# Fourteen loads of x, each issued as two transfers, of 108 and of 20 rows

## The chip, the core and the metric

The kernel runs on one core of one Trainium2 chip. The metric is the device time of one execution in microseconds (us). The kernel before takes 314.12 us, the median of three runs (314.06 to 314.76).

## What is computed

Attention over a small set of inducing points, and behind it a mixture step without a gate. All inputs and the output are float32.

```python
# x: (4, 12544, 128), inducing: (32, 128); scale = 1 / sqrt(128)
def mab(q, kv):
    a = softmax(scale * q @ kv.T)
    return a @ kv
h = mab(inducing, x[b])          # (32, 128) for each of the four batches
y = mab(x[b], h)                 # (12544, 128) for each batch
out = maximum(y @ w1, y @ w2) @ w_out      # w1, w2: (128, 1024), w_out: (1024, 128)
```

## The kernel before, in words

**Tiling.** A batch has 12544 rows of x, 98 for each of the 128 partitions. A tile `xn` holds 14 rows of x for each partition (14 x 128 values in float16), so a batch is seven tiles; there are 12 such buffers. `xT` is the same data turned, with the 128 channels on the partitions. In the text load (b, i) is part i of batch b. Batch 0 is cut finer: its parts hold 14, 14, 14, 14, 7, 7, 7, 7, 6, 4, 2 and 2 rows of x per partition. The later batches have seven parts of 14.

**Loads of x.** `load_x` (L213) issues a load from POOL (GpSimd), since the transfer also turns float32 into float16. One load moves 128 rows of the access pattern, one for each partition. Part (0, 0) alone comes over SP in float32 and is cast by DVE and ACT. POOL takes its instructions in order, and an issue is one of them. The framework counts landings with eight semaphores that it deals out to POOL's transfers in turn, so a transfer waits for the landing of the one issued eight before it, when that has not been waited for yet.

**The head (0 to about 25 us).** Only batch 0 is worked on. PE turns each part of x (L292), DVE and ACT copy the result to `xT` (L296, L299), PE makes scores (L308), ACT takes exp (L320), PE sums (L345, L354). Behind the loads of batch 0 POOL issues two halves of w1 and w2 (`relus<-in_moe_w_dram`, L269 and L270), then w_out (L271), and then the seven loads of batch 1. Between the loads of batch 1 stand three computations of POOL: `w21 = w2 - w1` for columns 256 to 511 (L576), the same for columns 512 to 767 (L576 again), and the cast of the second half of w1 to float16 (L585). Their code, in the order of issue:

```python
load_x(1, 0)
difference(nc.vector, 0, 256, 21.0, 0.34)
difference(nc.gpsimd, 256, 512, 21.0, 0.64)
load_x(1, 1)
load_x(1, 2)
difference(nc.gpsimd, 512, 768, 22.9, 0.64)
cast_w1(1)
for i in range(3, 7):
    load_x(1, i)
```

PE needs the first difference for `hwd` of columns 256 to 511 (L517), the second one for columns 512 to 1023 (L535, `rest_hwd`), and the cast for turning w1 (L598, `weights_2`). DVE makes the difference of the last 256 columns (also L576) before L535.

**The main part (about 25 us to the end).** The order of PE's work is a written list of words (`PLAN`), which is not changed by a late operand: PE stops at an instruction whose operand is missing. The large groups are the hidden products and their relu (PE L956, then DVE L900 or ACT L902), the products with w_out (PE L836), and the outputs, scaled by DVE (L871) and stored by SP (L885). In between, for batches 1 to 3, SP turns `xn` to `xT` by DMA (L227), PE and ACT make scores and exp (L385, L397), SP turns the exps (L415), PE sums (L430). POOL works out softmax denominators for some blocks (L697, L701) from exps that SP turned (L688).

**Later loads.** When the last sum of batch b is made, `load_x(b + 1, i)` is called for i = 0 to 6 in one go (L463 and on), the first behind a small copy (`pace`, L218) that makes POOL wait for that sum.

Of the kernel before, what the change touches and what calls it, by code (L numbers as in the profile page):

```python
# [144 lines left out]
def kernel(  # L145
# [9 lines left out]
    nc = tc.nc  # L155
    B, N, C = x.shape
# [20 lines left out]
    xr = x.rearrange("b (p k) c -> b p k c", p=128)  # L177
# [30 lines left out]
    xn_at = {}  # L208
    for b in range(B):
        for i, (k0, n) in enumerate(parts[b]):  # L210
            off = k0 % P1
            xn_at[b, i] = xn_tiles[(7 * b + k0 // P1) % NXN][:, off : off + n, :]

    def load_x(b, i, after=None):
        k0, n = parts[b][i]
        if after is not None:

            nc.gpsimd.tensor_copy(out=pace, in_=after)  # L218
        nc.gpsimd.dma_start(out=xn_at[b, i][:, 0:n, :], in_=xr[b, :, k0 : k0 + n, :])  # L219

    HALVES = 4
    turns_x = [(i, 7 * h, 7) for i in range(HALVES) for h in (0, 1)] + [(i, 0, P1) for i in range(HALVES, 7)]
# [31 lines left out]
    with tc.manual_schedule(engines={ET.PE, ET.DVE, ET.Activation, ET.Pool, ET.SP}):  # L254
# [3 lines left out]
        for lo, hi in ((0, 8), (8, P1)):  # L258
            nc.sync.dma_start(out=xf[:, lo:hi, :], in_=xr[0, :, lo:hi, :])
        nc.sync.dma_start(ind_sb, inducing)  # L260
        load_x(0, 1)
        make_identity(nc, identity16)
        load_x(0, 2)
        make_identity(nc, identity32)
        for i in range(3, len(parts[0])):
            load_x(0, i)
# [829 lines left out]
```

## Time and profile before

| | |
|---|---|
| Median of three runs | 314.12 us (314.06 to 314.76) |
| The profiled execution | 313.17 us, its span 311.4 us |
| PE, ACT, DVE, POOL busy | 98%, 88%, 87%, 41% of the span |
| DMA packets of POOL's transfers (queue q0) | 22.7% of 16 engines' span |
| DMA packets of SP's transfers (queue q1) | 56.3% of 16 engines' span |
| Granted TensorE clock, mean | 0.998 |

The span runs from the first to the last instruction; the profiled execution has 1.77 us around it. Engines are PE (TensorE), PEld (its weight loads), DVE (VectorE), ACT (ScalarE), POOL (GpSimd) and SP (SyncE). A row of a timeline has the start in us from the start of the span, the duration, engine, line, operation, output and inputs, the count of instructions merged into it, and in brackets how long the engine had been idle and what ended that. A DMA row of POOL shows the time that the issue takes on POOL, not the transfer.

### The profile page before, as it was taken

To read this page: it belongs to the slowest core of one execution; us is meant where nothing else is said; L and a number is where in the kernel's file an instruction comes from. 1 tells how busy PE (TensorE), PEld (TensorE's weight loads), DVE (VectorE), ACT (ScalarE), POOL (GpSimd) and SP (SyncE) were. 2 spreads that over 40 slices of the span, in tenths; PEclk is the share of its full clock that TensorE was granted. 3 is DMA by queue.
4 is the path that set the end of the run, shared out by engine and by line. 5 is a ranking of instruction groups with operands and counts; after the bars stand their busy time and mean duration, and the time that the engine had idled before them with its cause. 6 is when DMAs were issued, how large, how long until landed. Compare 5 with 4: busy or idle time off the path is not lost.

```text
span 311.4 us, 12499 instructions
## 1 busy us (share of the span) xinstructions
PE 305.2 (98%) x5306; PEld 239.8 (77%) x5306; DVE 271.0 (87%) x443; ACT 275.5 (88%) x485; POOL 127.0 (41%) x189
## 2 busy tenths in 40 slices
PE   8999999999999999999999999999999999999995
PEld 3876777778877787778777887687878877788885
DVE  2468999999889999999899888998999899999883
ACT  3669999998998989998999999998989899988884
POOL 7373001476610290568500890347023343297300
PEclk9999999999999999999999999999999999999999
DMA  8999999999599999998899999874422532334323
GB/s 207 208 262 200 200 253 179 201 217 213 116 225 244 223 251 192 165 211 241 168 245 215 242 230 237 179 155 139 137 86 103 138 96 98 108 138 120 113 93 121
DMA packets 81336, 55.81 MB, mean 179 GB/s; under 512 B 62816, under 2 KB 66176, under 8 KB 81280
## 3 DMA queue, kind: packets, MB, share of 16 engines
q1 hardware_dynamic: 75312, 41.32, 56.3%
q0 software_dynamic: 5968, 13.70, 22.7%
q8 instruction: 41, 0.67, 0.9%
q14 instruction: 15, 0.12, 0.1%
HBM read 27.28 MB, written 25.69 MB: 170 GB/s over the span
## 4 chain that ended last, share of the span: by engine, by line
PE 89%; DMA 6%; POOL 2%; DVE 2%; issue 1%; POOLq 0%; DVEq 0%
PE psall L836 60%; PE psall L956 22%; DMA xn<-in_x_dram 3%; DMA relus<-in_moe_w_dram 2%; PE psall L644 2%; PE psall L430 1%; PE psall L385 1%; DVE relus L900 1%; DMA eT<-eu 1%; POOL xn L219 1%; POOL w L576 1%; PE psall L546 0%; PE psall L469 0%; DVE m1bd L565 0%; PE psall L852 0%
## 5 line engine op out<-in xcount | busy, mean ns | idle before, releaser
L902 ACT ACTIVATE relus<-psall 128x512 f16<-128x512 f32 (+1 forms) x373 | 234.0, 713 | 21.6 <-PE psall L956 20.1
L900 DVE TENSOR_SCALAR relus<-psall 128x512 f16<-128x512 f32 (+1 forms) x265 | 194.4, 775 | 18.9 <-PE psall L956 17.8
L836 PE MATMUL psall<-woutp,relus 128*128 128x128 f16 x3104 | 202.0, 220 | 0.0
L836 PEld LDWEIGHTS <-relus 128*128 128x128 f16 x3104 | 174.9, 98 | 31.7 <-issue 26.9
L956 PE MATMUL psall<-e,hwd 32*128 32x512 f16 (+2 forms) x840 | 80.2, 362 | 0.2
L697 POOL TENSOR_TENSOR half<-ed 128x256 f32<-128x256 f16 (+2 forms) x23 | 14.1, 612 | 141.8 <-DMA ed<-e 141.7
L701 POOL TENSOR_TENSOR rd<-den,minus 128x16 f32<-128x16 f32 (+2 forms) x23 | 60.7, 2639 | 1.8
L871 DVE TENSOR_TENSOR osbs<-psall,rd 128x512 f32<-128x512 f32 (+2 forms) x85 | 53.9, 636 | 4.2 <-issue 1.1
L956 PEld LDWEIGHTS <-hwd 32*128 32x128 f16 x880 | 27.4, 91 | 15.7 <-issue 3.6
L956 PE MATMUL psall<-m,e 32*128 32x128 f16 x372 | 35.5, 217 | 0.0
L956 PEld LDWEIGHTS <-e 32*128 32x128 f16 x372 | 21.6, 92 | 5.6 <-issue 0.4
L697 POOL TENSOR_TENSOR half<-half 128x32 f32<-128x32 f32 (+4 forms) x69 | 22.3, 323 | 5.4
L219 POOL DMA_DIRECT2D xn<-in_x_dram x32 | 17.9, 574 | 5.2 <-DMA xn<-in_x_dram 3.7
L296 DVE COPY xT<-psall 128x512 f16<-128x512 f16 (+3 forms) x12 | 5.8, 486 | 8.6 <-PE psall L292 8.5
L871 DVE TENSOR_TENSOR osbs<-psall,rp 128x512 f32<-128x512 f32 (+3 forms) x20 | 12.7, 641 | 0.4 <-PE psall L956 0.3
L654 ACT ACTIVATE e<-psall 128x512 f16<-128x512 f32 (+2 forms) x21 | 10.9, 571 | 0.0
L397 ACT ACTIVATE eu<-psall 128x512 f16<-128x512 f32 x18 | 10.8, 619 | 0.0
L299 ACT COPY xT<-psall 128x768 f16<-128x768 f16 (+3 forms) x10 | 5.7, 574 | 4.4 <-PE psall L292 4.2
L292 PE MATMUL psall<-identity,xn 128*128 128x128 f16 x98 | 8.0, 227 | 0.4 <-DMA xn<-in_x_dram 0.4
L644 PE MATMUL psall<-xT,hT 128*32 128x512 f16 (+3 forms) x110 | 8.4, 362 | 0.0
L292 PEld LDWEIGHTS <-xn 128*128 128x128 f16 x98 | 6.0, 101 | 2.3 <-DMA xn<-in_x_dram 0.8
L385 PE MATMUL psall<-xT,inducingT 128*32 128x512 f16 x72 | 6.0, 382 | 0.0
(116 smaller groups left out, 127.3 us busy)
## 6 DMA issues: line engine op xcount, KB each, us to landing
out_dram<-osbs SPq DMA_DIRECT2D x90, 256.0 KB, 2.9
xn<-in_x_dram POOLq DMA_DIRECT2D x24, 448.0 KB, 9.8
out_dram<-osbs SPq DMA_DIRECT2D x10, 128.0 KB, 2.3
relus<-in_moe_w_dram POOLq DMA_DIRECT2D x4, 256.0 KB, 6.0
xn<-in_x_dram POOLq DMA_DIRECT2D x4, 224.0 KB, 9.6
xT<-xn SPq DMA_TRANSPOSE x33, 4.5
relus<-in_x_dram SPq DMA_DIRECT2D x1, 512.0 KB, 3.5
relus<-in_x_dram SPq DMA_DIRECT2D x1, 384.0 KB, 4.0
```

The costliest lines, as they stand in the source:

```text
L219: nc.gpsimd.dma_start(out=xn_at[b, i][:, 0:n, :], in_=xr[b, :, k0 : k0 + n, :])
L292: nc.tensor.transpose(ps[:, j, :], xn[:, g + j, :], identity16)
L397: nc.scalar.activation(out=eu, in_=ps, func=AF.Exp, scale=scale, accum_out=st[b]["es"][:, u : u + 1])
L644: nc.tensor.matmul(out=ps[32 * q : 32 * (q + 1), 128 * t : 128 * (t + n)], lhsT=hq, rhs=xT[:, c : c + n, :], start=True, stop=True, tile_p ...
L654: nc.scalar.activation(out=blk.e2[:, 0 : 128 * wd], in_=ps[:, 0 : 128 * wd], func=AF.Exp, scale=st[0]["rs"] if blk.b == 0 else scale,)
L697: nc.gpsimd.tensor_tensor(out=dst, in0=cur[:, :, 0:n], in1=cur[:, :, n : 2 * n], op=ALU.add)
L701: nc.gpsimd.tensor_tensor(out=rp[:, 0:wd, :].rearrange("p t q -> p (t q)"), in0=den[:, 0 : 4 * wd], in1=minus1[:, 0 : 4 * wd], op=ALU.pow,)
L836: nc.tensor.matmul(out=g.ps[:, 128 * t : 128 * (t + 1)], lhsT=home[:, 128 * (jb * w4 + t) : 128 * (jb * w4 + t + 1)], rhs=woutp[:, jb, :], ...
L871: nc.vector.tensor_mul(osb[:, 0:n, :], g.ps[:, 0 : n * C].rearrange("p (s c) -> p s c", s=n), blk.rp[:, 0:n, q : q + 1].broadcast_to((128, ...
L900: nc.vector.tensor_scalar(out=dst, in0=src, scalar1=0.0, scalar2=None, op0=ALU.max)
L902: nc.scalar.activation(out=dst, in_=src, func=AF.Relu)
L956: nc.tensor.matmul(**seq.pop(0))
```

## The change

Loads (0, 2), (0, 4) and (b, 0) to (b, 3) for b = 1, 2, 3 were one transfer of 128 rows (partitions 0 to 127). Now partitions 0 to 107 and 108 to 127 are two transfers. Those of (0, 4) have 7 x 128 values in a row, the other nine 14 x 128. Fourteen loads are split: two of batch 0 and four of each later batch. POOL issues 46 transfers of x where it issued 32; the bytes are the same.

```diff
+    SPLIT = {(0, 2), (0, 4)} | {(b, i) for b in range(1, B) for i in range(4)}
+
     def load_x(b, i, after=None):
         k0, n = parts[b][i]
         if after is not None:
 
             nc.gpsimd.tensor_copy(out=pace, in_=after)
-        nc.gpsimd.dma_start(out=xn_at[b, i][:, 0:n, :], in_=xr[b, :, k0 : k0 + n, :])
+        cut = 108 if (b, i) in SPLIT else 128
+        for p0, p1 in ((0, cut), (cut, 128)):
+            if p0 < p1:
+                nc.gpsimd.dma_start(out=xn_at[b, i][p0:p1, 0:n, :], in_=xr[b, p0:p1, k0 : k0 + n, :])
```

The change adds five lines above `load_x`'s end, so L576 of before is L581 of the change, and so on.

**Place one: POOL, between the loads of w_out and the last loads of batch 1 (19 to 26 us).** `xn7_91` to `xn1_85` are the seven loads of batch 1, `w21_103` is the difference of w2 and w1, `relus_80` the space in which the float32 weights lie, and DMASW0 to DMASW7 are the eight landing semaphores. Before:

```order
L278 MEMSET m1bd_107 128x512
L219 DMA xn7_91<-in_x_dram 128x1792 [waits DMASW0_49]
L576 TENSOR_TENSOR w21_103<-relus_80 128x256 [waits DMASW4_49,DMASW3_49]
L219 DMA xn8_92<-in_x_dram 128x1792 [waits DMASW1_49]
L219 DMA xn9_93<-in_x_dram 128x1792 [waits DMASW2_49]
L576 TENSOR_TENSOR w21_103<-relus_80 128x256 [waits DMASW6_49,DMASW5_49]
L585 COPY relus_80<-relus_80 128x512
L219 DMA xn10_94<-in_x_dram 128x1792
```

The same place in the change:

```order
L283 MEMSET m1bd_107 128x512
L224 DMA xn7_91<-in_x_dram 108x1792 [waits DMASW2_49]
L224 DMA xn7_91<-in_x_dram 20x1792 [waits DMASW3_49]
L581 TENSOR_TENSOR w21_103<-relus_80 128x256 [waits DMASW6_49,DMASW5_49]
L224 DMA xn8_92<-in_x_dram 108x1792 [waits DMASW4_49]
L224 DMA xn8_92<-in_x_dram 20x1792
L224 DMA xn9_93<-in_x_dram 108x1792
L224 DMA xn9_93<-in_x_dram 20x1792 [waits DMASW7_49]
L581 TENSOR_TENSOR w21_103<-relus_80 128x256 [waits DMASW0_49]
L590 COPY relus_80<-relus_80 128x512
```

Two issues stand ahead of the first difference where one stood, and four between the two differences where two stood. The cast follows the second difference as before.

**Place two: POOL, the loads of batch 2.** `xn2` to `xn8` with the numbers 86 to 92 are the seven loads. Before:

```order
L219 DMA xn6_90<-in_x_dram 128x1792 [waits DMASW3_49,PE_49]
L219 DMA xn7_91<-in_x_dram 128x1792 [waits DMAHW6_49,DMASW4_49,PE_49]
L219 DMA xn8_92<-in_x_dram 128x1792 [waits DMAHW1_49,DMAHW5_49,DMASW5_49,PE_49]
L697 TENSOR_TENSOR half_8_2191<-ed_8_2188 128x256 [waits DMAHW6_49]
```

The same place in the change, with the pair ahead of it:

```order
L224 DMA xn5_89<-in_x_dram 108x1792 [waits DMASW3_49,PE_49]
L224 DMA xn5_89<-in_x_dram 20x1792 [waits DMASW4_49]
L224 DMA xn6_90<-in_x_dram 128x1792 [waits DMASW5_49,PE_49]
L224 DMA xn7_91<-in_x_dram 128x1792 [waits DMAHW6_49,DMASW6_49,PE_49]
L224 DMA xn8_92<-in_x_dram 128x1792 [waits DMAHW1_49,DMAHW5_49,DMASW7_49,PE_49]
L702 TENSOR_TENSOR half_8_2201<-ed_8_2198 128x256 [waits DMAHW6_49]
```

With eleven issues instead of seven, the ninth to eleventh use a semaphore that an issue of the same batch has used, and so wait for that one's landing.

## The prediction

> **What bounds the kernel now.** I begin with the page's busy times, to see which engine has room.
>
> ```profile
> PE 305.2 (98%) x5306; PEld 239.8 (77%) x5306; DVE 271.0 (87%) x443; ACT 275.5 (88%) x485; POOL 127.0 (41%) x189
> ...
> q0 software_dynamic: 5968, 13.70, 22.7%
> ```
>
> PE is busy for 98% of the span, POOL for 41%, and the loads that the change touches are in queue q0. So a load can matter only where PE waits for what it brings, or for POOL, which issues it. The view of waits says where that is. Its columns are who waited for whom, the total in us, the times, the longest.
>
> ```profile
> POOL half L697 <- DMA ed<-e: 141.7, 16, 26.3
> ...
> POOL xn L219 <- DMA xn<-in_x_dram: 3.7, 3, 1.7
> ...
> PE psall L292 <- DMA xn<-in_x_dram: 0.4, 2, 0.2
> ...
> PE psall L535 <- POOL w L576: 0.3, 1, 0.3
> ...
> PE psall L430 <- DMA eT<-eu: 0.2, 1, 0.2
> ```
>
> PE's direct waits for loads of x are 0.4 us in all, those for POOL 0.3 us in one place, L535. After the head the one DMA that PE is seen to wait for is an exp turned by SP (L430, 0.2 us), not a load. The queue's own view has one wait of a turning of x for its load, the first, which has nothing behind it that PE needs soon:
>
> ```profile
> SPq L227 <- DMA xn<-in_x_dram: 23.9, 1, 23.9
> ```
>
> So I read the head, about 25 us long, in POOL's timeline.
>
> ```profile
> 9.82 0.53 POOL L219 DMA_DIRECT2D xn<-in_x_dram  x1 [1.62 <-DMA xn<-in_x_dram]
> 12.04 0.53 POOL L219 DMA_DIRECT2D xn<-in_x_dram  x1 [1.69 <-DMA xn<-in_x_dram]
> 13.11 0.54 POOL L269 DMA_DIRECT2D relus<-in_moe_w_dram  x1 [0.55 <-DMA xn<-in_x_dram]
> 14.19 0.54 POOL L270 DMA_DIRECT2D relus<-in_moe_w_dram  x1 [0.53 <-DMA xn<-in_x_dram]
> 16.38 0.54 POOL L269 DMA_DIRECT2D relus<-in_moe_w_dram  x1 [1.65 <-DMA xn<-in_x_dram]
> 17.36 0.54 POOL L270 DMA_DIRECT2D relus<-in_moe_w_dram  x1 [0.44 <-DMA xn<-in_x_dram]
> 18.27 0.92 POOL L271 DMA_DIRECT2D woutp<-in_moe_w_out_dram  x1 [0.38 <-DMA xn<-in_x_dram]
> 19.18 0.54 POOL L278 MEMSET m1bd<- 128x512 f16 x1
> 19.65 0.56 POOL L219 DMA_DIRECT2D xn<-in_x_dram  x1
> 20.83 0.89 POOL L576 TENSOR_TENSOR w<-relus 128x256 f16<-128x256 f32 x1 [0.63 <-DMA relus<-in_moe_w_dram]
> 21.67 1.10 POOL L219 DMA_DIRECT2D xn<-in_x_dram  x2
> 22.78 0.94 POOL L576 TENSOR_TENSOR w<-relus 128x256 f16<-128x256 f32 x1
> 23.68 0.60 POOL L585 CAST relus<-relus 128x512 f16<-128x512 f32 x1
> ```
>
> Each issue up to 18.27 waits for a landing eight transfers back. The first difference starts at 20.83, when the weights land. From there POOL is idle no more: two issues (1.10 us), the second difference, the cast. PE's and DVE's timelines beside it:
>
> ```profile
> 23.03 0.40 PE L644 MATMUL psall<-xT,hT 128*32 128x512 f16 x4
> 23.77 0.38 PE L535 MATMUL psall<-w,hT 128*128 128x512 f16 x1 [0.34 <-POOL w L576]
> 24.08 0.39 PE L956 MATMUL psall<-e_first,hwd 32*128 32x256 f16 x2
> 24.40 0.56 PE L598 MATMUL psall<-identity,relus 128*128 128x128 f16 x7
> ```
>
> ```profile
> 22.73 0.42 DVE L576 TENSOR_TENSOR w<-relus 128x256 f16<-128x256 f32 x1
> 24.26 0.75 DVE L523 TENSOR_SCALAR hwd<-psall,rs 128x512 f16<-128x512 f32 x1 [0.43 <-PE psall L535]
> ```
>
> PE has nothing left at 23.43 (23.03 + 0.40) and gets L535 at 23.77, 0.05 us after the second difference ends (22.78 + 0.94 = 23.72). DVE then waits for L535 (0.43 us idle). **So at this point POOL's string of issues sets the time of the whole kernel**, and the change puts two more issues into it.
>
> **The change part by part.**
>
> *Two more issues between the differences.* An issue of 128 rows costs 1.10 / 2 = 0.55 us there. Issues of 20 or 108 rows are not in the trace. Two rows bound them: an issue of 2-column loads (128 rows of 512 bytes, at 12.04) takes 0.53 like one of 14 columns, so bytes don't count; w_out, cut into 8 x 128 = 1024 pieces, takes 0.92, so 896 more pieces cost about 0.39 us, 0.0004 us each. By that 20 rows cost 0.53 - 108 x 0.0004 = 0.48 us and 108 rows 0.52. If the whole 0.53 followed the number of partitions, which the rows can't exclude because all of them have 128, a pair would cost what one does, and the addition would be nothing. I take the first, since w_out shows a fixed part: two pairs cost 2 x (0.48 + 0.52) = 2.0 in place of 1.1 us, **0.9 to 1.1 more, I take 1.0; the lower end is 0.** Nothing covers it: POOL has no idle time from 20.83 on, and PE's L535 comes straight behind.
>
> *The issue ahead of the first difference.* One more here, 0.5 us, is covered: POOL was idle for 0.63 us before 20.83. If the weights land earlier, the cover shrinks.
>
> *What a split does to the landing.* A load of 14 columns takes 12.04 - 9.82 = 2.22 us of the queue and one of 7 columns 14.19 - 13.11 = 1.08. But the next step, 16.38 - 14.19 = 2.19, is also one of 7 columns: it lands 1.11 us late. In that stretch (13.9 to 15 us) the view of DMA has a foreign packet:
>
> ```profile
> q0 software_dynamic: 135, 0.22, 107.2%
> q8 instruction: 1, 0.02, 5.5%
> ```
>
> One fetch of instructions, 5.5% of 16 engines' 1.1 us, is 0.97 us on one of them. A load has landed when all its engines are done, so one late engine makes every landing behind it late. A second such fetch stands at 19.3 to 20.4:
>
> ```profile
> q0 software_dynamic: 140, 0.41, 95.5%
> q8 instruction: 1, 0.02, 5.8%
> ```
>
> How the 108 and 20 rows fall on the 16 engines no row shows. With 128 rows it is eight for each, 2.22 / 8 = 0.28 us for a row of 14 columns and 0.135 for one of 7. If 108 rows go seven to an engine, the last one gets 3, and 20 rows go two to each of the first ten. The heaviest then have 9 rows, one more than before, 0.28 + 0.135 = 0.41 us for the two split loads of batch 0; the last has 3, which is 5 x (0.28 + 0.135) = 2.1 us less. If the last engine is the one that fetches, the 1.11 us of lateness go and 0.41 comes: landings are up to 0.70 us earlier. If a heavy one fetches, they are 0.41 later. The steps behind the late one, 0.98 (17.36 - 16.38) for 7 columns that should take 1.08, show that 0.1 or so is made up anyway. I take 0.4 us earlier for the weights, so the first difference at 20.43. POOL gets there: w_out starts with its landing, 0.4 earlier at 17.87, and w_out, the memset and two pieces take 0.91 (to 19.18) + 0.47 (to 19.65) + 1.0, which ends at 20.25. **Term: -0.4, between -0.7 and +0.4.**
>
> The skill's rule is another one. By the Trainium skill, "DMA: Bandwidth & Descriptors", section "Why a DMA increments its semaphore by 16 and not by 1", a transfer uses the largest number of engines up to 16 that divides its slowest dimension, so 12 for 108 rows and 10 for 20, but it notes that some direct copies issued by GpSimd are dealt over 16, rounded up, instead. No run here shows which holds; the first is a rival below, the second the case just worked out. The same page, section "Rules for kernel authors", advises against two transfers over disjoint halves of the partitions, since they share the same engines.
>
> *Before the first fetch.* (0, 2) and the loads up to (0, 5) land 0.28 to 0.41 us later, since no engine was late yet. PE turns them as they land, but it waits again for the late one behind 14.19, so this is made up there.
>
> *Later batches.* For batches 2 and 3 POOL issues eleven times in place of seven.
>
> ```profile
> 83.27 3.82 POOL L219 DMA_DIRECT2D xn<-in_x_dram  x7 [0.31 <-PE psall L956]
> 106.40 0.66 POOL L697 TENSOR_TENSOR half<-ed 128x256 f32<-128x256 f16 x1 [19.31 <-DMA ed<-e]
> ```
>
> Seven take 3.82 us; four more cost about 2.2, and the ninth to eleventh wait for landings of the same batch, the first of which comes 4.9 us after its issue:
>
> ```profile
> xn<-in_x_dram POOLq DMA_DIRECT2D x1, 448.0 KB, 4.9
> ```
>
> Behind them POOL is idle for 19.31 us, which hides all of it: nothing. Nor do earlier landings gain there, since no wait of PE for these loads stands in the view of waits. For batch 1 the last four loads are issued up to 3 us later; POOL's next work is at 52.75, a turned exp, so nothing again:
>
> ```profile
> 52.75 0.66 POOL L697 TENSOR_TENSOR half<-ed 128x256 f32<-128x256 f16 x1 [26.34 <-DMA ed<-e]
> ```
>
> **Sum.** +1.0 (issues) - 0.4 (first difference earlier) = +0.6 us at L535. From L535 on PE, DVE and ACT follow one another without a store of work, so I carry it to the end in full. The profiled execution, 313.17 us with a span of 311.4, would become 313.8; it lies 0.95 under the median of the runs shown, so on that scale 314.12 + 0.6 = 314.7.
>
> **The rivals.**
>
> *No help for the fetching engine (28%).* The landings stay or come up to 0.4 us later, and the issues cost 1.0 to 1.1: 315.1 to 315.6. For it: only one of the 16 engines gets as few as 3 rows. Against it: the lighter engines in between (7 rows) would help a little too.
>
> *Fewer engines for a transfer (12%).* If every engine of a transfer must get as many rows as the next, 108 rows go to 12 engines (9 each) and 20 to 10 (2 each). An engine that is in both has 9 + 2 = 11 rows, three more than eight: 0.83 us for (0, 2) and 0.41 for (0, 4), at most 1.24 if they fall on the same ones. The first difference slips by up to that, and the issues come on top: +1.0 to +2.2, about 316.0. This is the rule of the skill without its exception.
>
> *Faster (13%).* If an issue costs by its rows, a pair is as cheap as one, and the first difference starts 0.4 us or more earlier; then L535 starts when PE is done with L644, at 23.43 in place of 23.77. It decides at a pair's price: under 0.75 us (0.55 + 0.4 / 2), the second difference ends earlier than before. PE can't gain more than the 0.34 it waited, so 313.8. For it: no issue of fewer than 128 rows is in the trace. Against it: w_out's fixed part.
>
> *Much faster (5%).* Stalls that the views don't show, shorter than a product's own time on PE, could hang on late landings in the main part; 1 to 1.5 us would be 312.9. Against it: no wait for loads there.
>
> **How the numbers follow.** The forecast has 42%, and its own range is 314.3 (0.7 earlier, issues 0.9) to 315.1 (no gain). The predicted time is 314.7. For 8 in 10 I leave out the much faster case and the end of the dearest one: 313.7 to 315.9. A measurement here can tell 0.3% from no change, 0.94 us, so the bounds are 313.2 and 315.1. Slower than that: the fewer engines (12%), most of no help (24%), a corner of the forecast (4%), 40%. Faster: the much faster case and a sliver of the faster one, 6%. The rest, 54%, is within.
>
> **What would show it.** In POOL's timeline: four issues of about 2.0 us between the differences, the second one at about 23.4; the step of 2.19 us behind the first fetch shrunk to about 1.1; PE's idle time before L535 grown from 0.34 to about 1 us; and the rest of the kernel moved as a whole. I am wrong if a pair's issues take 0.55 us, if landings before 13 us come over 0.5 us later (fewer engines), or if the distance from L535 to the end changes by more than 0.3 us.

## The result: 315.87 us, and where the time went

The change takes **315.87 us** (median of 8 runs, 315.18 to 320.05) against 314.09 us of the kernel before beside it (8 runs, 313.53 to 314.76). The ratio is 1.0053, with a 95% interval of 1.0037 to 1.0068: slower by about half a per cent. Single runs near 320, 366 and 407 us at a lowered clock, of this kernel and of two below, are left out of the ratios.

The profiled execution took 315.83 us, so the pair of profiles differs by 2.66 us (313.17 before), 0.9 more than the medians. The page of the change:

```profile
span 314.0 us, 12518 instructions
...
PE 304.7 (97%) x5306; PEld 239.1 (76%) x5306; DVE 271.6 (87%) x443; ACT 275.4 (88%) x485; POOL 134.2 (43%) x203
...
PE 90%; DMA 4%; DVE 3%; SPq 1%; issue 1%; POOL 0%; ACT 0%; DVEq 0%; POOLq 0%
```

PE has done the same 5306 products in nearly the same time (304.7 us, 305.2 before), so the 2.6 us are PE's waits. The last row is the chain of work that ended last, by engine. SP's queue, which turns x and exp, has come into it with 1%. POOL had 2% in before and has 0% here, but that rests on a row that names the wrong engine, as shown below. Setting each instruction of DVE beside the same one of before shows where the distance grows: it is 0.73 us from 27 to 122 us, grows by 2.19 us between 118 and 128 us, loses 0.30 us near 213 us (where PE's wait for an exp at L430 is gone), and ends at 2.63.

**The first 0.73 us lie in the head.** POOL's timeline of the change, the rows that answer to those of before:

```profile
14.67 0.54 POOL L275 DMA_DIRECT2D relus<-in_moe_w_dram  x1 [0.32 <-DMA xn<-in_x_dram]
15.79 0.54 POOL L274 DMA_DIRECT2D relus<-in_moe_w_dram  x1 [0.57 <-DMA xn<-in_x_dram]
...
19.34 1.09 POOL L224 DMA_DIRECT2D xn<-in_x_dram  x2
20.52 0.92 POOL L581 TENSOR_TENSOR w<-relus 128x256 f16<-128x256 f32 x1
21.38 2.14 POOL L224 DMA_DIRECT2D xn<-in_x_dram  x4
23.54 0.91 POOL L581 TENSOR_TENSOR w<-relus 128x256 f16<-128x256 f32 x1
```

Four issues take 2.14 us where two took 1.10. The step of 2.19 us is 1.12 now (15.79 - 14.67), the first difference starts at 20.52 instead of 20.83, and the second at 23.54 instead of 22.78. PE's timeline of the change there:

```profile
23.61 0.40 PE L649 MATMUL psall<-xT,hT 128*32 128x512 f16 x4
24.50 0.38 PE L540 MATMUL psall<-w,hT 128*128 128x512 f16 x1 [0.49 <-DVE relus L905]
```

And DVE's timeline of the change:

```profile
23.30 0.57 DVE L581 TENSOR_TENSOR w<-relus 128x256 f16<-128x256 f32 x1
23.80 0.68 DVE L905 TENSOR_SCALAR relus<-psall 128x512 f16<-128x512 f32 x1
```

L540 starts at 24.50 against 23.77. The row names DVE's relu L905 as the releaser, which ended last (23.80 + 0.68 = 24.48). But L540 doesn't need it: in b2_only, a kernel with the same L540 below, that relu runs until 25.11 (24.43 + 0.68), and L540 starts before:

```profile
24.43 0.68 DVE L905 TENSOR_SCALAR relus<-psall 128x512 f16<-128x512 f32 x1
```

```profile
24.56 0.39 PE L540 MATMUL psall<-w,hT 128*128 128x512 f16 x1 [1.00 <-DVE w L581]
```

L540 needs the two differences. In the change DVE's ends at 23.87 (23.30 + 0.57) and POOL's at 24.45 (23.54 + 0.91), 0.05 us ahead of L540, as in before (23.72 and 23.77). So POOL's string sets L540 here too. PE had fallen behind as well (L649 at 23.61 against 23.03), because it waits longer for the first loads of x, but it still has to wait 0.49 us for POOL. The view of waits of the change shows the waits for x, and the larger loss too:

```profile
PEld L390 <- DMA xT<-xn: 1.8, 1, 1.8
...
PE psall L390 <- DMA xT<-xn: 1.6, 2, 1.3
PE psall L297 <- DMA xn<-in_x_dram: 1.5, 2, 0.8
```

L297, the turning of the first loads on PE, waits 1.5 us in place of 0.4.

**The other 2.19 us lie in batch 2**, where before had no wait in this profile. PE's scores of batch 2, in the kernel before:

```profile
122.80 0.62 PE L385 MATMUL psall<-xT,inducingT 128*32 128x512 f16 x8
```

and in the change, where the same eight products come in three pieces:

```profile
123.54 0.39 PE L390 MATMUL psall<-xT,inducingT 128*32 128x512 f16 x4
125.20 0.39 PE L390 MATMUL psall<-xT,inducingT 128*32 128x512 f16 x2 [1.27 <-DMA xT<-xn]
125.95 0.39 PE L390 MATMUL psall<-xT,inducingT 128*32 128x512 f16 x2 [0.36 <-DMA xT<-xn]
```

They wait for x turned by SP. SP's queue in the kernel before (start, us until the issues were through, count):

```profile
99.62 7.74 SPq L227 DMA_TRANSPOSE xT<-xn  x3
...
117.03 3.99 SPq L227 DMA_TRANSPOSE xT<-xn  x3
```

and in the change:

```profile
100.36 10.63 SPq L232 DMA_TRANSPOSE xT<-xn  x3
...
119.99 4.90 SPq L232 DMA_TRANSPOSE xT<-xn  x3
```

The first three turnings of batch 2 take 10.63 us in place of 7.74, and all that SP has behind them starts later. The middle one of the three behind 117.03, in a shorter window of before:

```profile
118.39 1.27 SPq L227 DMA_TRANSPOSE xT<-xn  x1
```

The view of DMA of before for the moment of its issue has the us from issue to landing:

```profile
xT<-xn SPq DMA_TRANSPOSE x1, 4.6
```

118.39 + 4.6 = 122.99, and the second four of the eight products, of which the last two need it, start at 123.02 in before. **There was no wait and no slack either: 0.03 us.** In another execution of the same program (before_again, below) there is a wait of 0.30 us at this place.

In the change this turning is issued at 121.37. Set against the first of the eight products (122.80 and 123.54), that is 2.24 us later than in before, and it takes 4.54 us to land. 2.24 - 0.06 (it lands that much sooner after its issue) - 0.03 (the slack) = 2.15, so that SP's lateness accounts for the 2.19 us.

The loads themselves end later. Counted from the first issue of batch 2 (83.27 in before, 84.01 in the change), the last load has landed at 105.54 - 83.27 = 22.27 us before and 108.18 - 84.01 = 24.17 in the change. Four loads are split, and the distance collects there: the fourth has landed after 14.15 us before and after 16.07 (its second piece) in the change. The first three turnings are through a little after that last load, 1.8 us in before (99.62 + 7.74 = 107.36 against 105.54) and 2.8 in the change (110.99 against 108.18); so in b2_only (1.5) and quad_skew (2.9) below.

### The profile page after: what moved, and what is told of

Its sections match the earlier page's. It is cut to its first block, busy times and chain, and to the rows that moved or that the text cites. A ratio compares the mean times of both kernels' runs of the same rounds, so it can differ in the third digit from the quotient of the medians.

```text
span 314.0 us, 12518 instructions
## 1 busy us (share of the span) xinstructions
PE 304.7 (97%) x5306; PEld 239.1 (76%) x5306; DVE 271.6 (87%) x443; ACT 275.4 (88%) x485; POOL 134.2 (43%) x203
## 4 chain that ended last, share of the span: by engine, by line
PE 90%; DMA 4%; DVE 3%; SPq 1%; issue 1%; POOL 0%; ACT 0%; DVEq 0%; POOLq 0%
PE psall L841 59%; PE psall L961 22%; DMA xn<-in_x_dram 2%; DVE relus L905 2%; PE psall L649 1%; PE psall L435 1%; DMA xT<-xn 1%; PE psall L297 1%; PE psall L390 1%; SPq L232 1%; PE psall L313 1%; PE psall L359 1%; PE psall L551 0%; PE psall L350 0%; PE psall L474 0%
## 5 line engine op out<-in xcount | busy, mean ns | idle before, releaser
L905 DVE TENSOR_SCALAR relus<-psall 128x512 f16<-128x512 f32 (+1 forms) x265 | 194.5, 775 | 18.5 <-PE psall L961 17.3
L224 POOL DMA_DIRECT2D xn<-in_x_dram x46 | 25.1, 551 | 14.6 <-PE psall L961 6.6
L297 PE MATMUL psall<-identity,xn 128*128 128x128 f16 x98 | 7.4, 219 | 1.8 <-DMA xn<-in_x_dram 1.5
L649 PE MATMUL psall<-xT,hT 128*32 128x512 f16 (+3 forms) x110 | 8.4, 362 | 0.0
L390 PE MATMUL psall<-xT,inducingT 128*32 128x512 f16 x72 | 6.6, 382 | 1.6 <-DMA xT<-xn 1.6
L297 PEld LDWEIGHTS <-xn 128*128 128x128 f16 x98 | 5.6, 97 | 3.1 <-DMA xn<-in_x_dram 1.7
```

What stands on the lines that cost most here:

```text
L224: nc.gpsimd.dma_start(out=xn_at[b, i][p0:p1, 0:n, :], in_=xr[b, p0:p1, k0 : k0 + n, :])
L297: nc.tensor.transpose(ps[:, j, :], xn[:, g + j, :], identity16)
L649: nc.tensor.matmul(out=ps[32 * q : 32 * (q + 1), 128 * t : 128 * (t + n)], lhsT=hq, rhs=xT[:, c : c + n, :], start=True, stop=True, tile_p ...
L905: nc.vector.tensor_scalar(out=dst, in0=src, scalar1=0.0, scalar2=None, op0=ALU.max)
```

## The experiments

Of the fourteen split loads thirteen have 14 x 128 values in a row, and (0, 4) has 7 x 128. My theory after the result: the head's extra issues cost what was predicted, and batch 2's loads end later because 108 rows give the busiest engine seven rows and 20 rows give it two, nine where eight would do. Rivals: each split as such costs time, with even rows too; rows fall on fewer engines; or the pair of profiles shows chance. The table gathers all runs. Times of before are medians of the runs of before that a kernel shared a chip with. L540 is the start of that product (L535 of before), "last load" the landing of batch 2's last load counted from its first issue, and "lost at L390" what PE's stream loses there against the first profile of before. These three come from one profiled execution each.

| kernel | us | before | ratio, 95% | L540 | last load | lost at L390 |
|---|---|---|---|---|---|---|
| before, first profile | 313.17 | | | 23.77 | 22.27 | 0 |
| the change | 315.87 | 314.09 | 1.0053 [1.0037, 1.0068] | 24.50 | 24.17 | 2.19 |
| b0_only | 314.13 | 314.29 | 0.999 [0.9969, 1.001] | 24.29 | 22.60 | 0.79 |
| b1_only | 314.86 | 314.29 | 1.0022 [0.9996, 1.0047] | 24.64 | 22.23 | 0 |
| b2_only | 315.48 | 314.29 | 1.0032 [1.0004, 1.006] | 24.56 | 23.55 | 1.15 |
| b3_only | 314.69 | 314.29 | 1.0004 [0.9977, 1.0031] | 24.80 | 22.42 | 0.15 |
| even_all | 315.12 | 314.13 | 1.0027 [0.9997, 1.0058] | 24.95 | 23.43 | 0.81 |
| even_b2 | 315.01 | 314.13 | 1.0008 [0.9979, 1.0037] | 24.65 | 23.46 | 0.81 |
| b1_late | 320.78 | 314.13 | 1.02 [1.0152, 1.0249] | 23.76 | 22.56 | 0.56 |
| prime_127 (one run) | 314.79 | 314.13 | | 24.61 | 22.44 | 0 |
| quad_even | 316.19 | 314.33 | 1.0045 [1.0011, 1.0079] | 24.65 | 23.81 | 0.71 |
| quad_skew | 318.6 | 314.33 | 1.0109 [1.0049, 1.017] | 24.67 | 26.14 | over 1.9 |
| memset_between | 314.28 | 314.33 | 0.998 [0.9952, 1.0008] | 24.18 | 22.34 | 0.77 |
| before_again (one run) | 314.68 | 314.33 | | 24.90 | 22.44 | 0.67 |

### The batches one by one

The split is kept for one batch alone.

```diff
-    SPLIT = {(0, 2), (0, 4)} | {(b, i) for b in range(1, B) for i in range(4)}
+    SPLIT = {(0, 2), (0, 4)}                  # b0_only
+    SPLIT = {(1, i) for i in range(4)}        # b1_only
+    SPLIT = {(2, i) for i in range(4)}        # b2_only
+    SPLIT = {(3, i) for i in range(4)}        # b3_only
```

**b0_only.** 

> Only the loads (0, 2) and (0, 4) are split. If the lengthened string of issues between the two differences is the loss of the head, this kernel loses none of it, since the extra issues lie where POOL waits for landings anyway: L535's counterpart no later than 24.1 us (before 23.8, the whole change 24.5), the time within -0.3 to +0.4 us of before. If the loss of the head came from the uneven rows of batch 0, L535 would be at 24.5 and the time +0.7 us.

Measured: 314.13 against 314.29, no difference. POOL's two differences in its profile:

```profile
21.34 0.89 POOL L581 TENSOR_TENSOR w<-relus 128x256 f16<-128x256 f32 x1 [0.59 <-DMA relus<-in_moe_w_dram]
...
23.30 0.94 POOL L581 TENSOR_TENSOR w<-relus 128x256 f16<-128x256 f32 x1
```

The weights land 0.5 us later than in the first profile of before, not earlier, so the gain of the prediction's second term is missing in this execution. L540 starts at 24.29, past the 24.1 expected, because the whole string started later.

**b1_only.** 

> Only batch 1 is split. Theory: two issues more between the differences, and no earlier landing of the weights to pay for them, so L535's counterpart 1.0 us later than before (24.8 us) and the time +1.0 us, with nothing more behind 30 us. Rival (the uneven rows of batch 0 make the loss of the head): L535 at 23.8 and no change of the time.

Measured: 314.86 against 314.29, +0.57, with an interval that touches 1. POOL's string in its profile:

```profile
21.68 2.15 POOL L224 DMA_DIRECT2D xn<-in_x_dram  x4
23.84 0.74 POOL L581 TENSOR_TENSOR w<-relus 128x256 f16<-128x256 f32 x1
```

PE's row behind it:

```profile
24.64 0.38 PE L540 MATMUL psall<-w,hT 128*128 128x512 f16 x1 [1.11 <-POOL w L581]
```

Here the string is at work without the cuts of batch 0: PE waits 1.11 us, for POOL. The mechanism of the first term is as predicted. On time its cost can't be told from nothing.

**b2_only.** 

> Only batch 2 is split. Theory: the loss of about 2 us near 125 us belongs to batch 2 alone (its loads end later, SP's turnings behind them are late, PE waits at L390): head as before, PE waits 1 to 2 us at L390 near 123 us, time +1.0 to +2.2 us. Rival (the wait at L390 is the delay of the head carried into another alignment): no wait there and no change of the time.

Measured: 315.48 against 314.29, +1.19, the only single batch whose interval stays off 1. PE's scores of batch 2:

```profile
124.96 0.39 PE L390 MATMUL psall<-xT,inducingT 128*32 128x512 f16 x4
125.58 0.39 PE L390 MATMUL psall<-xT,inducingT 128*32 128x512 f16 x2 [0.23 <-DMA xT<-xn]
126.34 0.39 PE L390 MATMUL psall<-xT,inducingT 128*32 128x512 f16 x2 [0.36 <-DMA xT<-xn]
```

The waits of the change are there with batch 2 split alone, smaller; with the weight loads' wait PE loses 1.15 us.

**b3_only.** 

> Only batch 3 is split. Both theories: its loads end about 1.5 us later, but no wait of PE hangs on them, so the time stays within 0.3 us of before. If a split costs wherever it stands, +1 to +2 us.

Measured: 314.69 against 314.29, not to be told from nothing. The medians of the four parts differ from before by -0.16, +0.57, +1.19 and +0.40 us, together 2.0; the whole has 1.78. Batch 2 is the largest part, and the only one clear of zero.

### Is it the uneven rows?

The cut goes to 112 and 16 rows, which is seven and one on each of 16 engines, for all splits (even_all) or for batch 2 (even_b2).

```diff
-        cut = 108 if (b, i) in SPLIT else 128
+        cut = 112 if (b, i) in SPLIT else 128
```

**even_all.** 

> All fourteen loads are split at partition 112 in place of 108: 112 rows are seven for each of 16 engines and 16 rows one for each, so no engine gets more than eight. The count of issues is that of the change. Theory (two terms: POOL's longer string in the head, and the uneven rows that make the loads of batch 2 end later): the head keeps +0.8 to +1.0 us, the last load of batch 2 lands about 22.3 us after the first issue as in the kernel before, no more wait at L390, time +0.6 to +1.0 us. Rival (the number of transfers makes batch 2 late): last landing at 23.5 to 24.2, time +1.5 to +1.8 us as in the change.

**even_b2.** 

> Only batch 2 is split, at partition 112. Theory (uneven rows): last landing of batch 2 about 22.3 us after the first issue, time within 0.3 us of before. Rival (number of transfers): last landing at 23.5 or later, time +1.0 us like the kernel with batch 2 split at 108.

Measured: 315.12 and 315.01 against 314.13. The last load of batch 2 lands at 23.43 and 23.46, as late as in b2_only (23.55) and 1.0 to 1.1 later than unsplit (22.39 on average of seven profiles, b1_late left out, 22.23 to 22.60). So **my theory of the uneven rows fell as the whole cause**: an even cut delays the loads too. On time these two can't be told from before, and at L390 they lose 0.81 us, hardly more than b0_only (0.79), memset_between (0.77) and before_again (0.67), which leave batch 2 whole.

Then the pieces were made more, even (quad_even) and very uneven (quad_skew), in batch 2 alone:

```diff
-        cut = 108 if (b, i) in SPLIT else 128
-        for p0, p1 in ((0, cut), (cut, 128)):
+        cuts = (0, 32, 64, 96, 128) if (b, i) in SPLIT else (0, 128)     # quad_even
+        cuts = (0, 17, 34, 51, 128) if (b, i) in SPLIT else (0, 128)     # quad_skew
+        for p0, p1 in zip(cuts, cuts[1:]):
```

**quad_even.** 

> Only the four loads (2, 0) to (2, 3) are cut, each into four transfers of 32 rows: two rows for each of 16 engines and transfer, eight in all, but 12 transfers more than in the kernel before (4 more in the kernels cut in two). If the number of transfers makes batch 2 end later (0.25 to 0.28 us each by the kernel cut at 112: 23.45 in place of 22.4 us), the last landing is 25.4 to 25.8 us after the first issue, and PE waits 2.5 to 3.5 us near 123 us. If only uneven rows cost, it is at 22.4.

**quad_skew.** 

> The same four loads in four transfers of 17, 17, 17 and 77 rows: 2 + 2 + 2 + 5 = 11 rows on the heaviest engine, three more than eight, with the same count of transfers as the kernel of four times 32. If uneven rows cost 0.28 us a row, the last landing is 4 x 3 x 0.28 = 3.4 us later than that kernel's; if rows cost little beside the number of transfers, it is within 1 us of it.

Measured: 316.19 and 318.6 against 314.33. With four even pieces the last load lands at 23.81, only 0.35 later than with two. So the delay isn't a price for each transfer, nor zero when the rows are even. Its profile loses 0.71 us at L390, though the time is 1.86 us over before. Where the rest goes that profile doesn't show; it is of one of the shorter executions of its kernel (315.58). With uneven pieces the busiest engine has 2 + 2 + 2 + 5 = 11 rows, three more than eight, four times; the last load lands 2.33 us later than in quad_even, 2.33 / 12 = 0.19 us for each such row. PE's scores in quad_skew:

```profile
127.35 0.61 PE L390 MATMUL psall<-xT,inducingT 128*32 128x512 f16 x2 [1.77 <-DMA xT<-xn]
```

It also loses about 1.4 us ahead of that, between 110 and 117 us, where a buffer `osbs` came free late behind SP's queue:

```profile
PE psall L961 <- DVE osbs L876: 1.2, 1, 1.2
```

So two things delay the loads: a split as such, 1.0 to 1.4 us over four loads (23.43 to 23.81 against 22.39), and uneven rows on top. By the 0.19 us, 108 and 20 rows add 4 x 0.19 = 0.76 us in batch 2; b2_only against even_b2 shows 0.09 and the change against even_all 0.74, so for 108 rows the price isn't settled.

**What all splits of batch 2 share is a late SP.** Counted as above, against the first of the eight products, the turning that before issues at 118.39 is late by 2.24 us in the change, 1.2 in b2_only, 0.9 in even_all, 0.7 in even_b2, 1.2 in quad_even and 3.4 in quad_skew. In the other seven profiles with batch 2 unsplit it lies between 0.23 early and 0.55 late. The loss at L390 is this lateness, plus what the turning takes to land beyond the 4.60 us of the first profile (it takes 4.09 to 4.97), less the 0.03, or nothing where that is below zero. That holds to 0.04 us in all these profiles but quad_skew's, where the clock fell at this place. So even cuts make SP late too, but by so little that the landing times of single turnings blur it: on average the unsplit profiles lose 0.37 us, the even cuts 0.78.

### How the rows fall on the engines

Only the first load of batch 3 is split, 127 rows and one.

```diff
+    SPLIT = {(3, 0)}
-        cut = 108 if (b, i) in SPLIT else 128
+        cut = 127 if (b, i) in SPLIT else 128
```

**prime_127.** 

> Only load (3, 0) is split, into 127 rows and 1. If a transfer's rows are dealt over 16 engines, rounded up (eight each, seven for the last), it lands 4.5 to 5.5 us after its issue like an unsplit first load (4.9). If the number of engines must divide the rows, all 127 rows are on one engine: 127 x 0.28 = 35 us or more to its landing, and PE or SP waits behind it.

The view of DMA at its issue, with the KB and the us from issue to landing:

```profile
xn<-in_x_dram POOLq DMA_DIRECT2D x1, 444.5 KB, 4.9
```

Unsplit, the first load of a batch landed after 4.9 us too. 127 rows on one engine would take 127 x 0.28 = 36 us. The first piece of 108 rows in the change's batch 2 lands sooner than 128 rows do:

```profile
xn<-in_x_dram POOLq DMA_DIRECT2D x1, 378.0 KB, 4.7
```

With nine rows on each of twelve engines it would land later than eight rows on sixteen. Both landings fit rows that are dealt to 16 engines and rounded up, and the rival of fewer engines is out. This is the exception that the Trainium skill notes in "DMA: Bandwidth & Descriptors", section "Why a DMA increments its semaphore by 16 and not by 1"; its rule by divisors doesn't hold for these loads.

### The head, from both sides

**b1_late** splits batch 1, but issues its loads behind the first two only after the two differences and the cast:

```diff
-        load_x(1, 1)
-        load_x(1, 2)
         difference(nc.gpsimd, 512, 768)
         cast_w1(1)
-        for i in range(3, 7):
+        for i in range(1, 7):
             load_x(1, i)
```

> Only batch 1 is split (at 108), and all loads from (1, 1) on are issued behind the cast of w1, so that only the pair of (1, 0) stands ahead of the first difference and nothing between the two differences. Theory (POOL's string of issues sets L535): L535's counterpart back at 23.4 to 23.9 us and the time back to that of before, within 0.3 us, though the same loads are split. Rival (the split loads of batch 1 cost through the DMA queues): +0.6 us like the kernel with batch 1 split in place.

Measured: 320.78 against 314.13, the dearest version, although L540 is back at 23.76. SP's queue in its profile:

```profile
30.87 12.94 SPq L232 DMA_TRANSPOSE xT<-xn  x1
43.85 2.18 SPq L888 DMA_DIRECT2D out_dram<-osbs  x2
```

And its view of waits:

```profile
DVE osbs L874 <- DMA out_dram<-osbs: 6.4, 1, 6.4
PE psall L959 <- DVE osbs L874: 5.8, 1, 5.8
```

One turning of x stands in SP's queue for 12.94 us (7.26 for the same one in before). A piece of a load of batch 1 lands as it ends, at 43.84, after a hole of 7.4 us without a landing; which of the two holds the other the trace doesn't say. The stores of results stand behind it, the buffers `osbs` run out, DVE waits 6.4 us for one, and PE 5.8. So to move these split loads behind the differences costs more than the issues between them do. Unsplit loads in that place were not tried.

**memset_between** takes the kernel before, and moves the memset of `m1bd` from ahead of the loads to a place between the loads and POOL's second difference, so that DVE's difference comes first:

```diff
-        nc.gpsimd.memset(m1bd, 0.0)
...
         load_x(1, 2)
+        nc.gpsimd.memset(m1bd, 0.0)
         difference(nc.gpsimd, 512, 768)
```

> No load is split; POOL's clearing of m1bd (0.47 us) moves from ahead of the load (1, 0) to between the load (1, 2) and the second difference, so that DVE's difference of the last 256 columns (0.42 us) always starts before POOL's. Theory (DVE and POOL exclude each other for these operations, and who comes first is chance: DVE first, L535 at 23.8 to 24.3; POOL first, DVE takes 1.65 us and L535 is at 24.6 to 24.8): L535 at 24.0 to 24.4 in every run, DVE's difference 0.4 to 0.6 us long, time 0 to 0.4 us under the median of before. Rival (no such exclusion, the string of POOL alone counts): L535 at 24.2 and time +0.4 us.

Measured: 314.28 against 314.33. DVE's difference takes 0.43 us, L535's counterpart starts at 24.18, and on time nothing can be told apart. Both the theory and its rival had L535 there, so the run doesn't tell them apart. No version here beats the kernel before.

**before_again** is the kernel before, unchanged, profiled in a second execution.

> The kernel before, unchanged, profiled once more. Theory (chance of who comes first): either like the first profile (DVE's difference 0.42 us, L535 near 23.8) or with DVE's difference near 1.65 us and L535 at 24.5 to 24.8, with a span 0.7 to 1 us longer. Without that chance the profile repeats within 0.3 us.

Measured: 314.68 beside 314.33. DVE's difference in this execution:

```profile
23.18 1.66 DVE L576 TENSOR_TENSOR w<-relus 128x256 f16<-128x256 f32 x1
```

POOL's, at the same moment:

```profile
23.24 0.76 POOL L576 TENSOR_TENSOR w<-relus 128x256 f16<-128x256 f32 x1
```

And PE's row behind both:

```profile
24.90 0.39 PE L535 MATMUL psall<-w,hT 128*128 128x512 f16 x1 [1.01 <-DVE w L576]
```

This execution of the same program loses 1.13 us at L535 and 0.67 at L385 against the first profile, and its span is 1.5 us longer. **The profile that I predicted from was an early one**: DVE's difference took 0.42 us there and 1.66 here.

## Why the prediction was right, and where it was not

The time, 315.87 us, lies in the range (313.7 to 315.9), but 0.03 us from its end, 1.2 above the 314.7, and above the forecast's own range (314.3 to 315.1). The range reached that high for the sake of dearer rivals, and what they describe isn't what happened, so that it holds the time is largely luck. The likeliest outcome, no change that can be told (54%), did not come. The forecast's mechanism was found in the profile; a second, larger one was missed.

*Two more issues between the differences: +1.0.* Right. 2.14 - 1.10 = 1.04 us, 0.535 for an issue on the average of two with 108 rows and two with 20.

*First difference 0.4 earlier.* Right in this profile, 0.31, where the late step has shrunk to 1.12 us. In b0_only, with the same splits of batch 0, the step is still 2.11 (17.05 - 14.94 in its POOL timeline) and the difference came 0.5 later. So the gain is luck of the execution. No view shows on which engine a fetch of instructions falls; that the gain hangs on it remains a guess. In the change the two terms give 1.04 - 0.31 = 0.73 us, which is what L540 is late.

*Before the first fetch: made up.* Wrong. PE's stream was still 0.58 behind at L649 (23.61), and 0.52 in b0_only (23.55). In the heads with batch 0 unsplit it is 0.10 to 0.46, so a good part of that isn't the split's. At L540 it costs nothing, since PE waits there for POOL all the same. But it covers part of that wait, which is 0.49 us in place of the 1 us that was named as a sign.

*Carried to the end in full.* Right for the pair: 0.73 stays 0.73 to 122 us. But before is mostly slower in the head than in its first profile. In nine profiles with the unsplit string of POOL, L535 stood at 23.77 to 24.90, and in seven of them at 24.56 or later, because DVE's difference had to wait. Against those the change's 24.50 costs nothing. The nine have 24.54 on average, and the three profiles with the longer string (the change, b1_only, even_all) 24.70. b0_only and b1_only, which hold all of the head's edits, show -0.16 and +0.57 us, neither apart from zero.

***Later batches: nothing.* This is the step that failed.** It said of the loads of batches 2 and 3 that POOL's idle time of 19.31 us "hides all of it". It hides the issues. It doesn't hide the landings: a split batch lands 1.0 to 1.9 us later, SP's turnings come through only after it, and PE uses one of them 0.03 us after it lands. I read "no wait in the view of waits" as room. The loss at L390 was 2.19 us in the profile of the change and 1.15 in b2_only; with batch 2 unsplit it was 0 to 0.79 (eight profiles, mean 0.37). The part that the change adds is so 0.8 to 1.8 us by these two profiles, and +1.19 by the median of b2_only. Of the medians' 1.78 us, most is this step and not the sum that was forecast. A sign of being wrong that the prediction named was met here: the distance from L535 to the end changed by 1.9 us (2.63 - 0.73), more than the 0.3.

*The rivals.* Fewer engines: out by prime_127, though 316.0 would have been nearest to the time. No help for the fetching engine: so it was in b0_only, but not in the change. A pair as cheap as one issue: out by the 0.535 us. Much faster: out by the time. The Trainium skill's advice against two transfers over disjoint halves of the partitions ("DMA: Bandwidth & Descriptors", "Rules for kernel authors") agrees with the sign; the runs add that an even cut into two already costs 1.0 us of landing.

*Open.* What of an even split delays the loads by 1.0 to 1.4 us, while four pieces cost hardly more than two, no run here settles. One thing was not tried by itself: with eleven issues the last one waits, for a landing of the same batch among others, and starts 9.65 us after the first (93.66 - 84.01), where before is through with all seven after 3.82. Other transfers of the queue are still under way then. The change loses 2.19 us at L390 and b2_only 1.15 because SP is later there by 1.0 us; the change's last load lands 0.62 later, and where the other 0.4 us come from is open.

## What to carry to other kernels

No wait in a trace is not slack: before you call a transfer hidden, set its landing, and that of what is turned or copied from it, beside the first use. A queue like SP's here hands a late load on to what stands behind it, stores included. Profile the kernel before twice, because a race between two engines can go the other way in the next execution, and a single page then shows a head that most executions don't have.

## What the hardware showed unexpectedly

**DVE and POOL shut each other out.** The two differences of w2 and w1 read two float32 operands each, on DVE and on POOL, at the same moment. When DVE gets in first it takes 0.42 us and POOL's takes 0.94; when POOL does, its difference takes 0.75 and DVE's 1.65, through POOL's cast (0.62) as well. Starts 0.05 us apart (22.73 and 22.78 in the first profile, 23.18 and 23.24 in before_again) went either way. The Trainium skill has the rule in "SBUF — State Buffer", section "Who interferes with whom": a DVE instruction with two SBUF inputs contends with a GpSimd one that reads SBUF, and the ports that the two share are an exclusive lock. The trace agrees, and shows that the block can last through two POOL instructions. Not all fits: in b1_only DVE's difference took 0.98 us from 22.91, and until 23.83 POOL had nothing but issues at work. What held it no row shows.

**Behind some waits of PE of about one microsecond its clock halved.** The view by stretches of b1_only has the stretch, its length, the busy us and count of PE, PEld, DVE, ACT and POOL, the granted clock, the DMA share and GB/s:

```profile
24.00:26.00 2.00, 1.32 (x15) 0.67 (x18) 1.37 (x3) 1.18 (x3) 2.00 (x4) 1.00 1.04 202
26.00:28.00 2.00, 2.00 (x26) 1.42 (x27) 2.00 (x5) 1.57 (x4) 1.29 (x3) 0.72 1.06 203
28.00:30.00 2.00, 2.00 (x23) 1.62 (x19) 1.20 (x3) 1.73 (x4) 0.53 (x1) 0.50 1.04 199
30.00:32.00 2.00, 2.00 (x36) 1.50 (x34) 1.29 (x4) 1.33 (x4) 0.00 (x0) 0.93 1.08 203
```

About two us after PE's wait of 1.11 us the clock falls to 0.50 for some 3.4 us (1.1 of the second stretch, all of the third, 0.3 of the fourth), and PE, 0.87 us behind the first profile of before at L540, is 2.28 behind at 31 us. So it was in b2_only (a wait of 1.00) and even_all (1.16), and in quad_skew at 127 us, at its wait of 1.77. It was not so in six others with 0.87 to 1.01 in the head, nor in four with 0.34 to 0.64. The Trainium skill, "TensorE: Matmul & The Clock Gate", section "What's actually happening", has the two clock states and a free-running window of about 3.4 us, and speaks of an idle window; the half clock and its 3.4 us agree, but here much less than a window of waiting came before it. Behind b1_late's wait of 5.8 us the clock was 0.53 from 50 to 56 us, so part of its 320.78 is that. That the wait is the cause was not tried by itself.
